# Three DMA queues for the loads of a Fourier stage, with other ring depths and pool assignments, in a Fourier, MoE and channel-mix kernel

## The chip, the cores and the metric

The kernel runs on one core of a Trainium2 chip. A core has a matrix engine (TensorE, in the profile PE, its weight loads PEld), a vector engine (VectorE, DVE), a scalar engine (ScalarE, ACT), GpSimd (POOL) and a sync engine (SyncE, SP). DMAs are issued from the instruction streams of SP, ACT or POOL; an issue sits in that stream in order, with the waits in front of it. The metric is the device time of one execution in microseconds (us), the lower the better.

## What is computed

The reference, cut to what matters (x is 4 x 3072 x 256, all in float32):

```python
X = rfft(x, axis=1)                          # along the 3072 positions
Yr = Xr @ w_r - Xi @ w_i + b_r               # 256 x 256 complex channel mix
Yi = Xr @ w_i + Xi @ w_r + b_i
Yr, Yi = soft_threshold(Yr, 0.01), soft_threshold(Yi, 0.01)
x = irfft(Yr + 1j * Yi, axis=1)              # float32
h = x @ w_in                                 # 256 -> 2048
x = (h - tanh(h)) @ w_out                    # 2048 -> 256
xk, xr = mu_k * x + (1 - mu_k) * x_prev, mu_r * x + (1 - mu_r) * x_prev
out = sigmoid(xr @ w_r2) * (relu(xk @ w_k) ** 2 @ w_v)
```

The MoE weights arrive in float64; the kernel converts them to float32 on the core.

## The kernel before

The program has three stages. The **transform** (the first fifth) does rfft, channel mix, threshold and irfft for four batches. The 3072-point transform is split into 96 x 32. For one batch it runs as follows, with the letters used below.

- **A**: eight tiles `x` (96 x 1024, 384 KB each, `load_x`) are multiplied with the 96-point matrix `f_sb`; ACT copies the result from PSUM into a tile `at` (line 464), which a DMA stores to DRAM as `adr` (line 467). In batch 0 the product is one plain float32 matmul per half tile, in the others three matmuls of split operands (`xa`, `xb`: high and low part).
- **q**: when all eight `adr` stores of the batch have landed, twelve loads `q` (256 KB, line 474) bring the rows back in the other order.
- **T, Y, V**: twelve units (`reg_unit`). T: 4 matmuls of `q` with the twiddle table `t` into bank `g`; ACT and DVE split the result into `xh`, `xl` (lines 344, 347, 499, 500). Y: 24 matmuls with the channel weights `wh`, `wl` into bank `y`; DVE adds the bias and thresholds (lines 524 to 529), ACT and DVE split that into `zh`, `zl`. V: 6 matmuls with the table `b` into bank `v`; ACT copies them to a tile `v` (line 548), and a DMA stores it as `vdr` (line 550).
- **P** (`reg_ap`): when all twelve `vdr` stores have landed, eight loads `vp` (line 557), 64 matmuls with `e_sb`, copies to `yt` (line 567) and stores `ydr` (line 568).

Beside the units DVE converts 16 weight blocks (`reg_conv`): load `raw` (512 KB, line 607), nine integer and float operations on DVE (lines 617 to 625), a store `wdr`. The second stage (**MoE**) loads these as `ws` (line 681) and makes from them operand forms `ah`, `al` (`reg_forms`, for `w_in`) and `wh`, `wl` (`reg_weight`, for `w_out`); the third stage is the channel mix over time. Both run from about 410 us to the end with PE nearly always busy.

Nothing reorders work on the chip: each engine runs its instructions in order. The order is made beforehand by a planner (`_Plan`), a list scheduler with a fixed cost per operation, a priority per operation (numbers of `K`) and one line for all DMAs (`nbytes / 360.0` ns). Dependences that are added to an operation by hand (`o.deps.add`) move its place in the planned order; the semaphore waits of the program are derived separately, from the tiles that it reads and writes. A tile is one of `bufs` buffers of a ring in a memory pool: a writer of the next tile waits for the users of the one `bufs` before. Pools open in order on reused memory: `px` (x, at, xa, xb) must be done before `pw` opens; `pt` (q, xh, xl, tables `t`, conversion scratch) before `q1`; `pm` before `q2`; `pl` (v, vp, yt) before `q3`. Before the change the forms of `w_in` blocks 0 to 3 lie in `pw`, `q1`, `q2`, `q3`.

A DMA takes one of eight semaphores of its kind in turn (DMAHW for SP and ACT, DMASW for POOL) and waits until the DMA eight before it has landed. In this kernel all loads and stores but the tables `b` are issued from SP.

Of the kernel before, what the change touches and what calls it, by code (L numbers as in the profile page):

```python
# [8 lines left out]
F32 = mybir.dt.float32  # L9
# [10 lines left out]
NP = 24  # L20
# [78 lines left out]
PACE = (0, 0, 1, 2, 3, 4)  # L99
XB, VB = 8, 4  # L100
# [47 lines left out]
class _Plan:  # L148
# [36 lines left out]
    def run(self):  # L185
# [54 lines left out]
        while done < len(ops):  # L240
# [70 lines left out]
def fourier_moe_kernel(tc, x, w_r, w_i, b_r, b_i, w_in, w_out, mu_k, mu_r, w_k, w_v, w_rr, c_f, c_e, c_t, c_b, out, nb=B, ydump=None):  # L311
# [67 lines left out]
    groups = [(0, 2), (2, 5), (5, 10), (10, 15), (15, 20), (20, NP)]  # L379
# [55 lines left out]
    def reg_a(b):  # L435
        for c in range(8):
            a = tile_(px, [NP * 4, 4, D], F32, "at", 3)
# [29 lines left out]
            dma("sp", lambda a=a, c=c: sp.dma_start(out=adr_t[b][:, 4 * c:4 * c + 4], in_=a()), pr, [adr[b]], [a], 393216)  # L467

    def reg_q(b):
        rows = adr_t[b].rearrange("r s d -> (r s) d").rearrange("(u k r) d -> u r k d", k=2, r=128)  # L470
        for u in range(NU):
            t = tile_(pt, [128, 2, D], F32, "q", NU)
            qt[b, u] = t
            dma("sp", lambda t=t, u=u: sp.dma_start(out=t(), in_=rows[u]), base(b) + u - K["q"], [t], [adr[b]], 262144)

    def reg_unit(b, u):
        n = 2
        z0 = base(b) + u
# [4 lines left out]
        qs = qt[b, u]  # L483
# [9 lines left out]
        op("pe", 448 * n, e, z0 - K["b"], [px_], [qs] + [t_sb[g] for g, _ in ts_])  # L493
        x3 = cut(px_, lambda r: r.rearrange("p (k c) -> p k c", k=4)[:, 0:2 * n])
# [52 lines left out]
        v = tile_(pl, [128, 2, D], F32, "v", 2)  # L547
# [41 lines left out]
    EARLY = 16  # L589

    def reg_conv(i):
        src, split = raws[i]
        if i < EARLY:
            w, q, s, l = (tile_(pt, [128, n], I32, tag, k) for n, tag, k in ((1024, "raw", 1), (512, "cq", 2), (512, "cs", 1), (512, "cl", 1)))
# [8 lines left out]
        def load():  # L603
# [3 lines left out]
            sp.dma_start(out=o, in_=src)  # L607
# [7 lines left out]
        dma("sp", load, pr, [raw[0]], [], 524288, after=[qt[0, NU - 1].writers[0] if i < EARLY else yload[int(K["l0"] + K["l1"] * (i - EARLY))]])  # L615
# [427 lines left out]
```

## Time and profile before

| | |
|---|---|
| median of 3 runs | 2035.78 us (2031.39 to 2036.15) |
| profiled execution | 2031.64 us, span in the trace 2029.9 us |
| PE busy | 1975.9 us (97%) |
| DVE, ACT busy | 1599.1 us (79%), 1479.3 us (73%) |
| DMA | 162.38 MB, of which about 98 MB in the first 400 us |

How to read it: a matmul that waits counts as idle time of PE, and its granted clock (PEclk, 1.00 is 2.4 GHz, 0.50 is 1.2 GHz) says how fast the busy time goes. PE is nearly always busy in the second and third stage, so what can move the time there is only the work itself. In the transform there are idle stretches and stretches at a lower clock.

### The profile page before, as it was taken

Reading aid. Unit: us, or ns where it says so; the run is one execution under the profiler, and the core shown is the slowest. Engines: PE = TensorE matmul, PEld = TensorE weight load, DVE = VectorE, ACT = ScalarE, POOL = GpSimd, SP = SyncE. Lnnn points to the kernel's source line nnn. Section 1 sums busy time; section 2 is a strip of 40 time slices with the busy share of each in tenths; the row PEclk is TensorE's granted clock in tenths of the full one; section 3 lists DMA queues with packets and bytes.
Section 4 is the critical chain, followed back from the end, with each engine's and each line's share of the span. In section 5 each row is a group of like instructions: output and inputs, shape, how many; then the busy total and the mean of one; then the engine's idle time right before and its main releaser. Section 6 shows DMA issues by size and latency. Waiting matters only on the chain.

```text
span 2029.9 us, 36670 instructions
## 1 busy us (share of the span) xinstructions
PE 1975.9 (97%) x13760; PEld 1834.6 (90%) x13760; DVE 1599.1 (79%) x3107; ACT 1479.3 (73%) x3166; POOL 3.7 (0%) x11
## 2 busy tenths in 40 slices
PE   5989999999999999999999999999999999999998
PEld 2989999888888888888888888888999999999998
DVE  0789875687888878787878797778988888888885
ACT  2647575677777777777777777778877777777774
POOL 0000000000000000000000000000000000000000
PEclk7999999799999999999999999999999999999999
DMA  9998865621101101010101020000111111112101
GB/s 246 276 288 276 293 217 163 186 72 34 37 28 41 46 26 37 21 48 22 48 22 37 21 84 32 22 11 23 58 47 47 47 46 47 48 47 55 49 22 32
DMA packets 98106, 162.38 MB, mean 80 GB/s; under 512 B 11559, under 2 KB 57735, under 8 KB 97927
## 3 DMA queue, kind: packets, MB, share of 16 engines
q1 hardware_dynamic: 97062, 156.89, 25.2%
q0 software_dynamic: 864, 3.15, 0.6%
q8 instruction: 108, 1.77, 0.4%
q14 instruction: 72, 0.58, 0.1%
HBM read 90.52 MB, written 69.47 MB: 79 GB/s over the span
## 4 chain that ended last, share of the span: by engine, by line
PE 87%; DMA 6%; DVE 4%; ACT 2%; issue 1%; SPq 1%; DVEq 0%; ACTq 0%
PE v L318 38%; PE y L318 19%; PE g L318 16%; PE a L318 14%; DMA vdr<-v 1%; DMA x<-in_x_dram 1%; DVE hs L831 1%; DVE hs L790 1%; DMA ydr<-yt 1%; DVE yl L347 1%; DMA out_dram<-ob 1%; DMA adr<-at 1%; DVE gl L347 1%; DMA yr<-ydr 0%; DMA q<-adr 0%
## 5 line engine op out<-in xcount | busy, mean ns | idle before, releaser
L344 ACT ACTIVATE gh<-hs 128x512 fp32r<-128x512 f32 x504 | 316.9, 629 | 138.8 <-PE v L318 130.4
L347 DVE TENSOR_TENSOR gl<-hs,gh 128x512 fp32r<-128x512 f32 x504 | 344.9, 684 | 78.5 <-ACT gh L344 77.6
L787 ACT ACTIVATE p<-g 128x256 f32<-128x256 f32 x864 | 318.5, 382 | 92.6 <-PE g L318 74.0
L831 DVE TENSOR_TENSOR hs<-hs,th 128x512 f32<-128x512 f32 x384 | 264.2, 689 | 124.0 <-ACT th L830 117.2
L318 PE MATMUL v<-gh,wl 128*128 128x512 f32 x768 | 302.9, 394 | 0.0
L318 PE MATMUL v<-gh,wh 128*128 128x512 f32 x768 | 302.2, 393 | 0.0
L318 PE MATMUL v<-gl,wh 128*128 128x512 f32 x768 | 301.2, 392 | 0.0
L830 ACT ACTIVATE th<-hs 128x512 f32<-128x512 f32 x384 | 241.1, 630 | 74.6 <-DVE hs L790 70.7
L790 DVE TENSOR_TENSOR hs<-y,p 128x256 f32<-128x256 f32 x588 | 241.5, 420 | 39.9 <-PE y L318 29.6
L318 PE MATMUL v<-ah,gh 128*128 128x256 f32 x768 | 217.4, 283 | 1.1 <-DVE ob L995 1.0
L318 PE MATMUL v<-al,gh 128*128 128x256 f32 x768 | 217.0, 283 | 0.0
L318 PE MATMUL v<-ah,gl 128*128 128x256 f32 x768 | 217.0, 283 | 0.0
L318 PE MATMUL g<-yh,ah 128*128 128x256 f32 x648 | 184.5, 285 | 1.5 <-ACT p L787 1.5
L318 PE MATMUL g<-yh,al 128*128 128x256 f32 x648 | 183.1, 282 | 0.0
L318 PE MATMUL g<-yl,ah 128*128 128x256 f32 x648 | 183.0, 282 | 0.0
L318 PEld LDWEIGHTS v<-gl,wh 128*128 128x128 f32 x768 | 144.3, 188 | 32.7
L318 PEld LDWEIGHTS v<-gh,wh 128*128 128x128 f32 x768 | 145.0, 189 | 17.9
L318 PEld LDWEIGHTS v<-gh,wl 128*128 128x128 f32 x768 | 144.7, 188 | 16.3
L318 PE MATMUL y<-yh,ah 128*128 128x256 f32 x496 | 150.2, 303 | 3.6 <-DVE hs L790 1.6
L318 PEld LDWEIGHTS v<-ah,gh 128*128 128x128 f32 x768 | 146.2, 190 | 1.7 <-DVE ob L995 1.7
L318 PEld LDWEIGHTS v<-al,gh 128*128 128x128 f32 x768 | 146.4, 191 | 0.0
L318 PEld LDWEIGHTS v<-ah,gl 128*128 128x128 f32 x768 | 146.2, 190 | 0.0
(171 smaller groups left out, 4884.6 us busy)
## 6 DMA issues: line engine op xcount, KB each, us to landing
x<-in_x_dram SPq DMA_DIRECT2D x32, 384.0 KB, 7.2
adr<-at SPq DMA_DIRECT2D x32, 384.0 KB, 3.6
q<-adr SPq DMA_DIRECT2D x48, 256.0 KB, 5.6
vdr<-v SPq DMA_DIRECT2D x48, 256.0 KB, 4.1
vp<-vdr SPq DMA_DIRECT2D x32, 384.0 KB, 5.7
ydr<-yt SPq DMA_DIRECT2D x64, 192.0 KB, 4.5
yr<-ydr SPq DMA_DIRECT2D x24, 512.0 KB, 4.1
xdr<-x SPq DMA_DIRECT2D x24, 512.0 KB, 3.1
```

The costliest lines, as they stand in the source:

```text
L318: pe.matmul(out=o, lhsT=l, rhs=r, start=st, stop=en, **kw)
L344: op("act", c_act(n, psum), lambda: act.activation(out=o[1](), in_=i[1](), func=ACTF.Copy), prio, [o[0]], [i[0]])
L347: op("dve", c_dve(n), lambda: dve.tensor_tensor(out=o[1](), in0=i[1](), in1=h[1]().bitcast(F32), op=ALU.subtract), prio, [o[0]], [i[0], h[0]])
L787: op("act", c_act(HK, True), lambda: act.activation(out=o(), in_=p()[:, 0:HK], func=ACTF.Copy), prio, [o], [p])
L790: op("dve", c_dve(HK), lambda: dve.tensor_tensor(out=t()[:, half * HK:half * HK + HK], in0=p()[:, 0:HK], in1=s(), op=ALU.add), prio, [t], ...
L830: op("act", c_act(CK, False), lambda th=th, hs=hs: act.activation(out=th(), in_=hs(), func=ACTF.Tanh), z0, [th], [hs])
L831: op("dve", c_dve(CK), lambda th=th, hs=hs: dve.tensor_tensor(out=hs(), in0=hs(), in1=th(), op=ALU.subtract), z0, [hs], [th])
```

## The change

- **Queues.** The loads of `w_r`, `w_i`, biases, `e_sb` and the tables `t` go from SP to POOL, beside the tables `b`. The `adr` stores of batch 0 go from SP to ACT. The raw loads of the 16 conversions go from SP to POOL.
- **Gates.** The planner holds each table load back by a matmul two units ahead (`first_mm`), and the first ones by readers of `x` tiles; the raw loads are held back until loads `q` of batches 1 to 3 instead of the last `q` of batch 0.
- **Order of units.** Unit 1 runs before unit 0 (unit 0 has four extra ACT operations). The table groups are cut accordingly.
- **Ring depths.** `x` 8 to 6 buffers, `at` 3 to 7, `v` 2 to 4.
- **Pools.** The conversion scratch moves from `pt` to `px`. The forms of `w_in` blocks 0 to 3 lie in `pw`, `pw`, `q1`, `q2`; the `w_out` blocks 0 to 2 in `pw` (before `q1`, `q1`, `q2`). Some later tiles move by one pool likewise.
- **Planner.** A DMA is planned at 290 instead of 360 bytes per ns.

```diff
-PACE = (0, 0, 1, 2, 3, 4)
-XB, VB = 8, 4
+XB, VB, AB = 6, 4, 7
+UNITS = (1, 0) + tuple(range(2, NU))
...
-                line = max(line, o.end + 650.0) + o.nbytes / 360.0
+                line = max(line, o.end + 650.0) + o.nbytes / 290.0
...
-    groups = [(0, 2), (2, 5), (5, 10), (10, 15), (15, 20), (20, NP)]
+    groups = [(2, 4), (0, 2), (4, 6), (6, 10), (10, 14), (14, 18), (18, NP)]
...
-        t = tile_(pl, [128, 2, D], F32, "v", 2)
+        t = tile_(pl, [128, 2, D], F32, "v", 4)
...
-        dma("sp", lambda t=t, w=w: sp.dma_start(out=t(), in_=w.rearrange(...)), -90, [t], [], 262144)
+        dma("pool", lambda t=t, w=w: pool.dma_start(out=t(), in_=w.rearrange(...)), -90, [t], [], 262144)
...
-        dma("sp", lambda: sp.dma_start(out=t_sb[n](), in_=c_t[:, g0:g1]), g0 / 2 - 60 + n, ...)
+        dma("pool", lambda: pool.dma_start(out=t_sb[n](), in_=c_t[:, g0:g1]), g0 / 2 - 60 + n, ...)
...
-            a = tile_(px, [NP * 4, 4, D], F32, "at", 3)
+            a = tile_(px, [NP * 4, 4, D], F32, "at", AB)
...
-            dma("sp", lambda a=a, c=c: sp.dma_start(out=adr_t[b][:, 4 * c:4 * c + 4], in_=a()), pr, ...)
+            q_, e_ = ("sp", sp) if b else ("act", act)
+            dma(q_, lambda a=a, c=c, e_=e_: e_.dma_start(out=adr_t[b][:, 4 * c:4 * c + 4], in_=a()), pr, ...)
...
-            w, q, s, l = (tile_(pt, [128, n], I32, tag, k) for ...)
+            w, q, s, l = (tile_(px, [128, n], I32, tag, k) for ...)
...
-            sp.dma_start(out=o, in_=src)
+            (pool if i < EARLY else sp).dma_start(out=o, in_=src)
...
-        dma("sp", load, pr, [raw[0]], [], 524288, after=[qt[0, NU - 1].writers[0] if i < EARLY else ...])
+        dma("pool" if i < EARLY else "sp", load, pr, [raw[0]], [], 524288, after=[qt[divmod(RAW0 + i * RAW1 // 4, NU)].writers[0] if i < EARLY else ...])
...
-        load_b[n].deps.add(xt[0, PACE[n]][0].readers[0])
-        if n > 1:
-            load_t[n].deps.add(qt[0, (groups[n][0] - 4) // 2].writers[0])
...
+                p = UNITS.index(g0 // 2)
+                for o, c in ((load_t[n], 4), (load_b[n], 6)):
+                    o.deps.add(first_mm[0, p - 2] if p > 1 else xt[0, c][0].readers[0])
...
-        win[q] = reg_forms((pw, q1, q2, q3)[q], str(q), 2 * q, P2 - K["win"] + 2 * q)
+        win[q] = reg_forms((pw, pw, q1, q2)[q], str(q), 2 * q, P2 - K["win"] + 2 * q)
...
-            wout[i] = reg_weight((q1, q1, q2, q2, q2, q3, q3, q3)[i], 8 + i, P2 - K["wout"] + 2 * q)
+            wout[i] = reg_weight((pw, pw, pw, q2, q2, q2, q3, q3)[i], 8 + i, P2 - K["wout"] + 2 * q)
```

Three places of the new order. First the start. The last rows of SP's loads before, down to the first loads `q` (the eight `x` and `w_r`, `w_i`, biases stand ahead of them; `t_147`, `t_152` are the first two tables `t`):

```order
L410 DMA e_sb<-in_c_e_dram 96x96
L415 DMA t_147<-in_c_t_dram 128x256
L415 DMA t_152<-in_c_t_dram 128x384
L467 DMA adr<-at 96x1024
L407 DMA bias<-in_b_i_dram 64x256
L409 DMA bias_137<-in_b_i_dram 63x256
L467 DMA adr<-at 96x1024 x7
L474 DMA q<-adr 128x2x256 x6
```

In the changed kernel SP from its first load on:

```order
L385 DMA f_sb<-in_c_f_dram 96x128
L398 DMA x<-in_x_dram 96x1024 x8
L475 DMA q<-adr 128x2x256 x12
L555 DMA vdr<-v 128x2x256
L396 DMA x<-in_x_dram 96x1024 x6
```

ACT in the changed kernel, from the first copy of A on (`wh` is made of `w_r`):

```order
L464 ACTIVATE at<-a 96x512 x2
L468 DMA adr<-at 96x1024
L464 ACTIVATE at<-a 96x512 x9
L468 DMA adr<-at 96x1024 x2
L424 ACTIVATE wh<-v 128x2x256
L468 DMA adr<-at 96x1024 x2
```

And POOL in the changed kernel, the end of its table loads and the first raw loads, with their waits:

```order
L417 DMA b_525<-in_c_b_dram 128x1024 [waits DMASW1_49]
L415 DMA t_535<-in_c_t_dram 128x512 [waits DMASW2_49]
L417 DMA b_628<-in_c_b_dram 128x1536 [waits DMASW3_49]
L415 DMA t_636<-in_c_t_dram 128x768 [waits DMASW4_49]
L613 DMA raw<-in_moe_w_in_dram 128x1024 [waits DMASW5_49]
L613 DMA raw<-in_moe_w_in_dram 128x1024 [waits DMASW6_49,DMASW5_49,DVE_49]
```

The stores stand in ACT's stream now, the first behind the first tile, the second behind eleven half tiles; the loads `x` of batch 1 stand behind the first `vdr` store. The table loads wait for the turn of their semaphore only, not for a matmul; the raw loads after the first one wait for DVE, which empties their one buffer.

Second, PE from the last A of batch 3 on. Before (the numbers are buffers):

```order
L318 MATMUL a_3156<-xb_3135,fh_106 128x512
L318 MATMUL y_3118<-wh_168,xh_2994 128x256 x4
L318 MATMUL y_3118<-wl_170,xh_2994 128x256 x4
L318 MATMUL y_3118<-wh_168,xl_2996 128x256 x4
L318 MATMUL v_3180<-zh_3138,b10_157 128x256 x2
L318 MATMUL v_3180<-zl_3146,b10_157 128x256
```

In the changed kernel, from the last block of Y down to the first T (`g`) of batch 3; between the last A and this fence stand one V (6 matmuls) and another block of Y:

```order
L319 MATMUL y_3244<-wh_180,xh_3143 128x256 x4
L319 MATMUL y_3244<-wl_185,xh_3143 128x256 x4
L319 MATMUL y_3244<-wh_180,xl_3159 128x256 x4
L319 MATMUL v_3291<-zh_3280,b18_628 128x256 x2
L319 MATMUL v_3291<-zl_3287,b18_628 128x256
L319 MATMUL v_3291<-zh_3280,b18_628 128x256 x2
L319 MATMUL v_3291<-zl_3287,b18_628 128x256
L319 MATMUL v_3330<-zh_3315,b18_628 128x256 x2
L319 MATMUL v_3330<-zl_3324,b18_628 128x256
L319 MATMUL v_3330<-zh_3315,b18_628 128x256 x2
L319 MATMUL v_3330<-zl_3324,b18_628 128x256
L319 MATMUL g_3345<-t2_163,q_3295 128x128 x4
```

Before, seven blocks of 12 Y and three V stand between the last A and the first T; now two blocks of 12 Y and three V (of 6 matmuls each).

Third, ACT at the end of the transform. Before, from the last copy but one into `v` on (`ah_4229`, `ah_4339` are forms of `w_in` blocks 1 and 2, `wh_4312` and `wh_4336` of `w_out`; `p`, `hs` belong to the first MoE products):

```order
L548 ACTIVATE v<-v 128x512
L344 ACTIVATE zh<-t 128x512
L344 ACTIVATE ah_4229<-ws 128x256
L787 ACTIVATE p_4287<-g 128x256
L787 ACTIVATE p_4302<-g 128x256
L344 ACTIVATE ah_4229<-ws 128x256
L344 ACTIVATE wh_4312<-ws 128x512
L548 ACTIVATE v<-v 128x512
L344 ACTIVATE ah_4229<-sq 128x1024
L344 ACTIVATE wh_4336<-ws 128x512
```

In the changed kernel, where six more units are still to deliver their `zh` (`ah_3941` is block 1, `wh_3960` of `w_out`; `zh`, `xh`, `xl` are unit work):

```order
L345 ACTIVATE zh<-t 128x512
L572 ACTIVATE yt<-a 128x384
L345 ACTIVATE ah_3941<-ws 128x256
L345 ACTIVATE yh<-yr 128x512
L345 ACTIVATE wh_3960<-ws 128x512
L345 ACTIVATE ah_3941<-ws 128x256
L345 ACTIVATE xh<-g 128x4x128
L345 ACTIVATE yh<-yt_3862 128x1024
L553 ACTIVATE v<-v 128x512
```

The forms of block 1 moved from between the last copies of the transform to between its units; those of block 2 stand now where those of block 1 stood.

## Rows read from the trace of the kernel before

**Rows 1.** The page, part 1: busy us per engine and its share.

```profile
PE 1975.9 (97%) x13760; PEld 1834.6 (90%) x13760; DVE 1599.1 (79%) x3107; ACT 1479.3 (73%) x3166; POOL 3.7 (0%) x11
```

**Rows 2.** Busy time in wide stretches: stretch, length, PE, PEld, DVE, ACT, POOL, PEclk, DMA, GB/s.

```profile
60.00:200.00 140.00, 133.54 (x1008) 127.46 (x1007) 122.01 (x237) 90.36 (x190) 0.00 (x0) 0.98 0.91 278
200.00:400.00 200.00, 189.37 (x1448) 184.50 (x1446) 138.76 (x263) 120.53 (x258) 0.00 (x0) 0.93 0.68 218
400.00:1400.00 1000.00, 997.50 (x6149) 887.54 (x6148) 811.02 (x1559) 765.05 (x1616) 0.00 (x0) 1.00 0.11 37
```

**Rows 3.** The same by 10 us, the stretches with losses.

```profile
120.00:130.00 10.00, 5.90 (x31) 5.71 (x30) 7.08 (x15) 4.25 (x12) 0.00 (x0) 0.70 0.85 305
...
290.00:300.00 10.00, 7.51 (x53) 7.31 (x53) 8.44 (x17) 6.93 (x17) 0.00 (x0) 0.83 0.94 328
...
360.00:370.00 10.00, 9.09 (x75) 8.68 (x73) 8.59 (x19) 6.23 (x16) 0.00 (x0) 1.00 0.49 156
370.00:380.00 10.00, 7.05 (x32) 6.18 (x33) 8.89 (x17) 8.48 (x20) 0.00 (x0) 0.66 0.85 248
380.00:390.00 10.00, 10.00 (x49) 10.00 (x49) 4.77 (x11) 4.91 (x12) 0.00 (x0) 0.50 0.76 218
390.00:400.00 10.00, 10.00 (x60) 9.98 (x59) 4.62 (x9) 5.48 (x12) 0.00 (x0) 0.64 0.77 253
```

**Rows 4.** Timeline of the start: start us, us, engine, line, operation, count, idle before.

```profile
1.25 3.32 POOL L417 DMA_DIRECT2D b<-in_c_b_dram  x6 [0.31 <-issue]
...
13.68 1.96 PE L318 MATMUL a<-x,f_sb 96*128 96x512 f32 x4 [1.04 <-DMA x<-in_x_dram]
...
24.76 0.33 SPq L467 DMA_DIRECT2D adr<-at  x1
...
29.60 10.13 PE L318 MATMUL a<-x,f_sb 96*128 96x512 f32 x16 [13.97 <-ACT at L464]
...
43.42 2.94 SPq L474 DMA_DIRECT2D q<-adr  x6
...
46.20 3.79 PE L318 MATMUL g<-t,q 128*128 128x128 f32 x16 [6.46 <-DMA q<-adr]
...
51.83 1.01 PE L318 MATMUL y<-wh,xh 128*128 128x256 f32 x3 [1.64 <-ACT xh L504]
```

**Rows 5.** Chain of work around 105 to 125 us: start us, us, what.

```profile
105.94 1.45 PE y L318 x12
107.38 0.72 PE v L318 x6
...
117.25 6.01 DMA vdr<-v
...
124.79 2.07 PE g L318 x8
```

**Rows 6.** Waits of ACT, 60 to 340 us: total us, times, longest.

```profile
ACT v L548 <- DMA vdr<-v: 7.9, 5, 3.5
```

**Rows 7.** Chain of work around 375 us.

```profile
376.12 1.65 PE g L318 x6
```

**Rows 8.** Loads of tile b, issued by POOL.

```profile
DMA to landing us min/median/max: 5.8/13.2/20.9
```

**Rows 9.** Tile raw: reads by DVE, who waited, landing.

```profile
L611 DVE TENSOR_SCALAR cq<-raw x16: 412/426/428, 74.5 to 244.2; 128x512 int32<-128x512 int32 x16
...
  DVE cq L611: 15.8, 9
...
DMA to landing us min/median/max: 4.2/5.9/7.0
```

**Rows 10.** Issues of adr and q, 255 to 292 us.

```profile
L474 SPq DMA_DIRECT2D q<-adr x12: 359/416/938, 282.8 to 291.4; - x12
L467 SPq DMA_DIRECT2D adr<-at x7: 303/398/821, 254.8 to 278.5; - x7
...
DMA to landing us min/median/max: 3.0/5.4/5.9
```

More of the change, by code (lines that the diff above doesn't have):

```diff
@@ L466, in reg_a, with reg_unit @@
                 op("act", c_act(512, True), v, pr, [a], [p], seq=False)
-            dma("sp", lambda a=a, c=c: sp.dma_start(out=adr_t[b][:, 4 * c:4 * c + 4], in_=a()), pr, [adr[b]], [a], 393216)
+            q_, e_ = ("sp", sp) if b else ("act", act)
+            dma(q_, lambda a=a, c=c, e_=e_: e_.dma_start(out=adr_t[b][:, 4 * c:4 * c + 4], in_=a()), pr, [adr[b]], [a], 393216)
     def reg_q(b):
         rows = adr_t[b].rearrange("r s d -> (r s) d").rearrange("(u k r) d -> u r k d", k=2, r=128)
-        for u in range(NU):
+        for i, u in enumerate(UNITS):
             t = tile_(pt, [128, 2, D], F32, "q", NU)
-            qt[b, u] = t
-            dma("sp", lambda t=t, u=u: sp.dma_start(out=t(), in_=rows[u]), base(b) + u - K["q"], [t], [adr[b]], 262144)
-    def reg_unit(b, u):
+            qt[b, i] = t
+            dma("sp", lambda t=t, u=u: sp.dma_start(out=t(), in_=rows[u]), base(b) + i - K["q"], [t], [adr[b]], 262144)
+    first_mm = {}
+    def reg_unit(b, pos):
         n = 2
-        z0 = base(b) + u
+        u = UNITS[pos]
+        z0 = base(b) + pos
         px_ = bank("g")
@@ L593, in reg_conv @@
         if i < EARLY:
[L594 removed]
+            w, q, s, l = (tile_(px, [128, n], I32, tag, k) for n, tag, k in ((1024, "raw", 1), (512, "cq", 2), (512, "cs", 1), (512, "cl", 1)))
             raw, q, s, l = (w, lambda: w().rearrange("p (c t) -> p c t", t=2)), (q, q), (s, s), (l, l)
@@ L613, in ts @@
                 dve.tensor_scalar(out=o, in0=i_, scalar1=s1, scalar2=s2, op0=o0, op1=o1)
-        dma("sp", load, pr, [raw[0]], [], 524288, after=[qt[0, NU - 1].writers[0] if i < EARLY else yload[int(K["l0"] + K["l1"] * (i - EARLY))]])
+        dma("pool" if i < EARLY else "sp", load, pr, [raw[0]], [], 524288, after=[qt[divmod(RAW0 + i * RAW1 // 4, NU)].writers[0] if i < EARLY else yload[int(K["l0"] + K["l1"] * (i - EARLY))]])
         c1, c2 = c_dve(512, False), c_dve(512)
@@ L641, in fourier_moe_kernel @@
     reg_q(0)
-    for n in range(len(groups)):
-        load_b[n].deps.add(xt[0, PACE[n]][0].readers[0])
-        if n > 1:
-            load_t[n].deps.add(qt[0, (groups[n][0] - 4) // 2].writers[0])
     for b in range(nb):
-        for u in range(NU):
-            reg_unit(b, u)
+        for i in range(NU):
+            reg_unit(b, i)
+        if b == 0:
+            for n, o in enumerate(early):
+                o.deps.add(xt[0, 1 + n][0].readers[0])
+            for n, (g0, _) in enumerate(groups):
+                p = UNITS.index(g0 // 2)
+                for o, c in ((load_t[n], 4), (load_b[n], 6)):
+                    o.deps.add(first_mm[0, p - 2] if p > 1 else xt[0, c][0].readers[0])
         if b + 1 < nb:
@@ L751, in reg_t @@
         pr = P2 + 8 * c - K["t"]
-        own = pw if c % 2 == 0 else q2
+        own = pw if c % 2 == 0 else q1
         y = tile_(pw, [128, 2, CK], F32, "yr", 1)
```

29 lines of the change are left out of this document (15 added, 14 removed).

## The prediction, made before the changed kernel had run

> **What bounds the kernel now.** I read the busy line of the page first [rows 1]: PE is busy for 1975.9 of 2029.9 us, so 54 us are idle, and those are the most that better waiting can give, beside a clock that is granted below 1.00. Then the stretches [rows 2, 3]: from 400 to 1400 us PE's busy time lacks 2.5 us of 1000, and the change leaves the order of that work nearly as it was. What can move lies in the first 400 us. There the losses stand in four places.
>
> The start: the fourth tile of A is multiplied from 13.68 on, then PE waits until 29.60, because the ring `at` has three buffers and SP issues the first `adr` store only at 24.76, behind every other load in its stream; the first `q` load is issued at 43.42 and T begins at 46.20 [rows 4]. 60 to 360 us: PE is idle for 6.5 us until 200 and 10.6 from 200 to 400, less 0.9 and 2.95 at 360 to 380: 13.2 us [rows 2, 3]. One of these is spelled out in the chain: a `vdr` store of 6.01 us ends, then PE's T begins at 124.79, after the 4.1 idle us of that stretch [rows 3, 5]; ACT stood at the copy into `v`, whose ring of two was full, and waited so for 7.9 us in all [rows 6]. The clock after such gaps: 0.70 at 120 and 0.83 at 290, which costs 5.90 x 0.30 + 7.51 x 0.17 = 3.0 us [rows 3]. The end of the transform: at 370 to 380 PE is idle for 2.95 us, the clock falls to 0.66, then 0.50 and 0.64 at full busy time: 7.05 x 0.34 + 5.0 + 3.6 = 11.0 us, with 3.9 idle 14.9 [rows 3]. There the chain runs through ACT without a gap, weight forms `ah` and `wh` among it, until PE's next product at 376.12 [rows 7].
>
> **The change part by part.** *Start, three queues.* The stores of batch 0 no longer stand behind other loads, and seven `at` buffers let PE go on. What sets T now is bytes. Before, four `x` tiles had arrived by 13.68, 3.1 us each from 1.25, 126 GB/s (384 KB each), while POOL moved 3.15 MB of `b`, the last issued at 4.0 and landing 20.9 us later, 133 GB/s [rows 4, 8]. Both queues share some 259 GB/s evenly. At that share the sixth tile is there at 19.9; then the seven stores that stand behind it, 2.75 MB, take 21 us at half of the rate (end at 41) or 10.6 at the whole (30.5). I take the middle, 35, as POOL's early loads are small ones: the first `q` 8.4 us earlier than 43.42 (bounds 2.4 and 13). The gates of the table loads cost and save nothing: in the new order they wait for semaphores of POOL alone, so they run as fast as the eight semaphores let them, as the six `b` loads did at 1.25 to 4.6, although they had hand-made gates too [rows 4]. *Unit 1 first*: before, Y waited 1.64 us for the four extra ACT operations of unit 0 and went on at 51.83 [rows 4]; unit 1 runs in that gap. -1.6.
>
> *The x loads of batch 1* stand behind the first `vdr` store. After the first V there are 3.9 us of PE work (three T, two of which took 3.79 us at the low clock [rows 4] and half of that at the full one, and parts of V) before A needs `xa`, `xb`; copy, two issues, a landing of 3.1 and two splits need about 5.6. +1.7 (0 to 6, if the tile lands as late as 7 us). Queued behind that wait on PE is the whole unit work, so it counts in full.
>
> *Rings and raw loads, 60 to 360 us.* With four `v` buffers ACT waits for the store four units back, some 18 us at 4.5 per unit (two blocks of Y at 1.45, V at 0.72, T at some 0.95); the stores take up to 6.01 [rows 4, 5]. ACT's 7.9 us of waiting there go [rows 6], and with them the PE gaps behind ACT. The raw loads leave SP; POOL has nothing else to do and refills the one buffer as soon as it is read, so DVE's 15.8 us of waiting for `raw` [rows 9] should shrink. Of 13.2 + 3.0 = 16.2 us I leave 3 (bounds 0 and 8: what is late next is the round trip `vdr` to `vp`). -13.2.
>
> *The new order opens one gap.* From the last A of batch 3 to its first T lay seven blocks of 12 Y (1.45) and three V (0.72), 12.2 us; now two and three, 5.0 us [rows 5]. The round trip was: last store issued at 278.5, first `q` at 282.8, landing 5.4 later [rows 10], 9.7 us, 10.3 with the copy. The gap is 5.3 us; with the quick landing at the start (43.42 to 46.20) and a 3.0 us store it is 1.8 [rows 4, 10]. I take 4.5, and for the clock the 1.8 us that 120 to 130 showed at a gap of that size [rows 3]. +6.3.
>
> *Pools, end of the transform.* The second `w_in` block and three `w_out` blocks now have room before the units end, and the order puts their forms between the units, where ACT and DVE have gaps. Between the last V and the first P stand 8.4 us of PE work instead of 3.2 (products of the MoE at about 0.12 and 0.23), against the same round trip of about 9. But ACT's list in that stretch still sums to some 9.5 us, so it stays late by a little, and a low clock can follow short gaps too, as it did here [rows 3]. Of 14.9 us I take 8.9 (bounds 0 and 14.9). Cover for the forms is the units of batch 3; if it is not there they are late at the old place.
>
> *Nothing*: fewer `x` buffers (A of the next batch is spread over the batch, each tile needs one), 290 instead of 360 in the planner (only the order), conversions nine units later (same density beside the units: 24 units, 30 half tiles of A and two P in either order).
>
> **Sum:** -8.4 - 1.6 + 1.7 - 13.2 + 6.3 - 8.9 = -24.1 us, 2031.6 - 24.1 = 2007.5 against the profiled execution. That lies near the low end of the three runs, 4.1 below their median; for a median I add half of that, and so in the rivals: **2009.5**.
>
> **The rivals.** *A, bytes and not queues.* If the tables get their share of the line until they are all in, 11.8 MB (x 3.15, `adr` 3.15, `b` 3.15, `t` 1.57, weights and biases 0.8) pass before `q`: at 259 GB/s that is 45.6 us, `q` at 46.8, 3.4 us later than before instead of 8.4 earlier: 2021. For it: both queues had equal shares [rows 4, 8]. Against: the stores have a queue of their own. The Trainium skill, page DMA: Bandwidth & Descriptors, section Issuing engines are not separate DMA queues, says that DMAs of all issuers run on the same engines, and that several issuers save only issue time. The rows agree as far as 259 GB/s in sum go, and by that rule alone the start is this rival.
>
> *B, the end stays*: ACT remains the late one and the clock falls as before; 8.9 us are not won: 2018. For it: the clock fell in a stretch whose gaps were short.
>
> *C, all of it*: start 13, no gap at batch 3, no remainder, end 14.9: about 46 us, 1988.
>
> *D, slower: raw loads on POOL land late.* There is one buffer, and DVE runs in order, so a late block stops the units. Conversions followed each other every (244.2 - 74.5) / 15 = 11.3 us [rows 9]; less three reads of 0.42, about 10 remain. They landed in 5.9 us from SP; the `b` loads from POOL took 5.8 to 20.9, in the middle 13.2 [rows 8, 9]. At 13.2, 16 x 3.2 = 51 us of DVE waiting, of which its idle time of 18 in 140 us [rows 2] takes some 20: +31, 2040, slower than before. It decides from a landing of about 12.8. Against: the `b` loads were six in a queue, the raw loads go one at a time. The Trainium skill, page SBUF — State Buffer, section SBUF: two separate sides, warns that DVE in a two-port mode keeps GpSimd from writing descriptors, and that a DMA of about 620 ns alone took about 3100 ns. No row of the kernel before shows POOL beside a busy DVE; worked out from that page, an estimate, a landing of 5.9 would become 8.4 and still be in time.
>
> *E, start and end both fail*: A and B together, 2030, no change that can be told.
>
> **How the numbers follow.** Forecast 0.46, A 0.13, B 0.15, C 0.08, D 0.09, E 0.09. A difference of under 0.3% (6 us) can't be told from none. Faster: 0.46 + 0.13 + 0.15 + 0.08 = 0.82; same: E, 0.09; slower: D, 0.09. The range reaches from 1992, which leaves out most of C, to 2030, which takes in A, B and half of E.
>
> **What would show it.** Right: first `adr` store near 8 us, first `q` at 30 to 41, T right behind; no wait of ACT for `vdr`, none of DVE for `raw`; a gap of 2 to 5 us before the first T of batch 3; the end of the transform at a clock near 1.00. Wrong: `q` after 43 (A); a clock of 0.50 for 20 us around the last P (B); raw landings over 10 us and DVE waiting for them (D); or a gap at a place that I don't name, such as the round trip `vdr` to `vp` in batches 0 to 2, or ACT standing at an `adr` issue.

## The result, and the profile after

The changed kernel takes 2008.1 us, median of four runs (2006.93 to 2009.99); the kernel before took 2033.59 beside it (2030.95 to 2036.15). The ratio is 0.9876, 95% interval 0.9857 to 0.9894. The forecast was 2009.5 in a range of 1992 to 2030. The profiled execution takes 2006.93 us (span 2005.1), 24.7 us less than the profiled one of before (2031.64).

The sum was right; its parts were not. To see that, I use one account for all kernels: for each stretch of 10 us the idle time of PE plus its busy time times (1 minus the granted clock), summed to 410 us. It gives 64.7 us before and 37.2 after. In all fourteen kernels the span less this account lies between 1960 and 1970 us, so it is good to about 5 us. It is read from one execution of each kernel, the profiled one. By places, before and after: the start (0 to 60 us) 33.1 and 27.5, the middle (60 to 250) 12.5 and 1.7, batch 3 and its surroundings (250 to 340) 4.2 and 5.6, the end of the transform (340 to 410) 14.9 and 2.4.

The busy line of the changed kernel's page, against [rows 1]:

```profile
PE 1961.8 (98%) x13760; PEld 1822.3 (91%) x13760; DVE 1599.4 (80%) x3107; ACT 1476.9 (74%) x3166; POOL 22.9 (1%) x42
```

The wide stretches of the changed kernel, against [rows 2]; from 400 us on nothing moved, as forecast:

```profile
60.00:200.00 140.00, 138.47 (x1074) 132.67 (x1073) 112.99 (x208) 94.10 (x201) 4.31 (x7) 1.00 0.84 265
200.00:400.00 200.00, 193.18 (x1524) 186.54 (x1523) 161.54 (x321) 129.48 (x282) 5.86 (x8) 0.99 0.71 227
400.00:1400.00 1000.00, 997.83 (x6133) 887.20 (x6132) 817.58 (x1567) 768.21 (x1621) 0.00 (x0) 1.00 0.11 35
```

Stretches of 10 us, against [rows 3]. The loss at 120 is gone, one has opened at 270, and the clock at the end of the transform stays at 1.00:

```profile
120.00:130.00 10.00, 10.00 (x89) 10.00 (x87) 8.90 (x19) 5.14 (x11) 0.53 (x1) 1.00 0.87 251
270.00:280.00 10.00, 6.76 (x46) 6.02 (x45) 9.96 (x22) 3.06 (x5) 0.72 (x1) 0.93 0.86 259
280.00:290.00 10.00, 9.04 (x70) 8.85 (x69) 5.54 (x11) 4.45 (x12) 0.72 (x1) 0.90 1.07 386
...
370.00:380.00 10.00, 9.53 (x83) 9.37 (x83) 6.89 (x15) 7.26 (x17) 0.00 (x0) 1.00 0.94 310
380.00:390.00 10.00, 9.92 (x79) 9.43 (x79) 4.61 (x10) 6.76 (x18) 0.00 (x0) 1.00 0.45 166
```

The start, against [rows 4]: the first `adr` store goes out 16.8 us earlier, `q` 7.0 and T 6.5 us earlier, and POOL issues all tables and then the first raw load by 24.97:

```profile
7.96 0.35 ACTq L468 DMA_DIRECT2D adr<-at  x1
...
24.97 0.53 POOL L613 DMA_DIRECT2D raw<-in_moe_w_in_dram  x1
36.39 7.71 SPq L475 DMA_DIRECT2D q<-adr  x12
...
39.72 3.61 PE L319 MATMUL g<-t,q 128*128 128x128 f32 x16 [16.17 <-DMA q<-adr]
```

ACT has no row any more that waits for `vdr` between 60 and 340 us (7.9 us in [rows 6]). DVE still waits for `raw`, 6.4 us instead of 15.8 [rows 9], and the raw loads land in 6.2 us from POOL (median; 5.9 from SP). The waits of DVE, 60 to 340 us: total us, times, longest:

```profile
DVE cq L617 <- DMA raw<-in_moe_w_in_dram: 3.3, 2, 2.6
DVE cq L617 <- DMA raw<-in_moe_w_out_dram: 3.1, 1, 3.1
```

Up to here everything looks as the prediction told it. The experiments say otherwise.

### The profile page after: what moved, and what is told of

Its sections match the earlier page's. It is cut to its first block, busy times and chain, and to the rows that moved or that the text cites. A ratio compares the mean times of both kernels' runs of the same rounds, so it can differ in the third digit from the quotient of the medians.

```text
span 2005.1 us, 36620 instructions
## 1 busy us (share of the span) xinstructions
PE 1961.8 (98%) x13760; PEld 1822.3 (91%) x13760; DVE 1599.4 (80%) x3107; ACT 1476.9 (74%) x3166; POOL 22.9 (1%) x42
## 4 chain that ended last, share of the span: by engine, by line
PE 89%; DVE 5%; DMA 3%; ACT 2%; issue 1%; SPq 0%; ACTq 0%; DVEq 0%
PE v L319 39%; PE y L319 20%; PE g L319 17%; PE a L319 14%; DVE hs L840 1%; DVE hs L799 1%; DVE yl L348 1%; DMA x<-in_x_dram 1%; DMA adr<-at 1%; DVE gl L348 1%; DMA ydr<-yt 0%; DMA out_dram<-ob 0%; DVE zl L348 0%; DMA vp<-vdr 0%; DMA yr<-ydr 0%
```

## The experiments

Each job also ran the kernel before; "difference" is the median less that median. The ratio and its interval come from all runs and not from the medians, so a few longer runs move them (e1). "V to P" is PE work, in us at full clock, that the order puts between the last V and the first P of batches 0 to 3, worked out as in the prediction; it covers the trip from `vdr` to `vp`, the store of the last V and the load behind it, and is called the cover below. The account is by the four places named above; for e5 the profiled execution (2035.2 us) lies 9 us above the median, for e10 (2008.08) 5 below it.

| kernel | median us | difference | ratio, interval | V to P | account, sum |
|---|---|---|---|---|---|
| before | 2033.59 | | | 7.9, 10.8, 7.9, 3.2 | 33.1 12.5 4.2 14.9, 64.7 |
| after | 2008.1 | -25.5 | 0.9876 (0.9857 to 0.9894) | 11.1, 18.3, 16.4, 8.4 | 27.5 1.7 5.6 2.4, 37.2 |
| e1 pools back | 2009.03 | -23.0 | 0.9908 (0.9876 to 0.9939) | 11.1, 18.3, 20.4, 4.5 | 29.7 3.1 8.3 4.4, 45.4 |
| e2 `v` ring 2 | 2009.62 | -22.4 | 0.9892 (0.9872 to 0.9911) | 12.2, 17.2, 17.2, 7.3 | 26.2 8.7 2.6 2.8, 40.4 |
| e3 raws on SP | 2008.01 | -24.0 | 0.988 (0.9862 to 0.9899) | 10.4, 16.1, 16.4, 7.3 | 27.2 2.9 5.5 2.5, 38.1 |
| e4 tables held | 2010.45 | -21.5 | 0.9895 (0.9876 to 0.9914) | 11.1, 18.3, 16.4, 8.4 | 30.3 3.4 5.2 2.5, 41.4 |
| e5 rate 360 | 2025.87 | -7.1 | 0.9972 (0.9947 to 0.9997) | 9.3, 8.6, 9.3, 6.3 | 23.5 17.7 11.3 14.7, 67.2 |
| e6 before, rate 290 | 2011.28 | -21.7 | 0.989 (0.9868 to 0.9912) | 18.6, 11.1, 18.3, 4.5 | 29.9 10.7 2.2 6.9, 49.8 |
| e7 start back | 2010.38 | -22.6 | 0.9891 (0.987 to 0.9913) | 14.0, 15.7, 15.8, 6.6 | 29.1 7.5 2.7 4.0, 43.3 |
| e8 start only | 2015.19 | -17.7 | 0.9908 (0.9883 to 0.9933) | 10.4, 9.3, 12.5, 3.2 | 20.0 8.9 2.2 16.2, 47.3 |
| e9 360, `vp` later | 2012.36 | -23.0 | 0.9898 (0.9863 to 0.9933) | 12.5, 12.5, 13.3, 10.8 | 26.1 10.3 1.9 4.1, 42.5 |
| e10 three parts back | 2012.70 | -22.6 | 0.989 (0.9862 to 0.9919) | 13.6, 15.0, 24.0, 4.5 | 29.5 5.3 5.1 6.1, 46.0 |
| e11 before, `v` ring 4 | 2045.30 | +10.0 | 1.0046 (1.0028 to 1.0064) | 7.9, 7.9, 8.3, 3.2 | 31.8 30.7 3.9 12.0, 78.4 |
| e12 mixed rate | 2002.72 | -28.9 | 0.986 (0.9844 to 0.9877) | 11.1, 18.3, 16.4, 8.4 | 22.1 2.0 5.2 2.0, 31.4 |

### One part undone at a time: e1 to e4

e1 puts the pools of conversion scratch and weight forms back:

```diff
-        win[q] = reg_forms((pw, pw, q1, q2)[q], ...)
+        win[q] = reg_forms((pw, q1, q2, q3)[q], ...)
```

> The changed kernel (2008.1 us) with the pool moves undone: conversion scratch in pt, forms of w_in in pw, q1, q2, q3, of w_out in q1, q2, q3, the later tiles likewise; all else as changed. Theory: the end of the transform ran at full clock only because the second block of forms was made between the units. Undone, ACT is late again at the last V, PE gets gaps of 2 to 5 us there and a clock of 0.5 to 0.7 for some 20 us: plus 8 to 14 us, 2016 to 2022. Rival: the gaps and the clock went for another reason (other order by the planner's 290, conversions elsewhere): 2006 to 2011, clock near 1.00 around the last P.

e2 puts the `v` ring back to 2, e3 the raw loads back on SP:

```diff
-        v = tile_(pl, [128, 2, D], F32, "v", 4)
+        v = tile_(pl, [128, 2, D], F32, "v", 2)
```

```diff
-            (pool if i < EARLY else sp).dma_start(out=o, in_=src)
+            sp.dma_start(out=o, in_=src)
```

> The changed kernel with the v ring back at 2 buffers. Theory: ACT stands at the copy into v for stores of vdr again, 5 to 10 us in all, PE waits behind it at the batch ends with a lower clock after: plus 5 to 12 us, 2013 to 2020. Rival: it was the raw loads leaving SP that freed the stores; then ACT's wait for vdr stays under 2 us and the time at 2007 to 2011. (The planner moves the first T of batch 2 closer to its last A, 6.5 instead of 11.5 us; a wait of T for q there would show as such.)

> The changed kernel with the 16 raw loads of the conversions issued from SP as before the change, same gates. Theory: DVE waits for raw blocks some 10 to 16 us in all instead of 6.4, part of it under the saturated stretch at 250 to 290: plus 1 to 4 us, 2009 to 2012. Rival: the queue is worth more, since SP's stores and loads stand behind them again: plus 6 or more, 2014 and up. Rival 2: nothing, 2008.

e4 adds a POOL operation ahead of the later table loads that waits for ACT's last copy of A in batch 0, so that the tables can't move before:

```diff
+                    op("act", 100, lambda: act.activation(out=gsink(), in_=gate(), func=ACTF.Copy), pr, [gsink], [gate], after=[plan.ops[-1]])
+                    op("pool", 100, lambda: pool.memset(gate(), 0.0), -58, [gate])
```

> The changed kernel with the table loads from the fourth group on really held back: a small POOL instruction in front of them waits for ACT's last copy of A in batch 0 (about 24 us). Theory that bytes set the start: 3.5 MB fewer stand beside the stores of A, the first q goes out at 26 to 31 instead of 36.4, T begins at 29 to 34 instead of 39.7, and the time falls by 4 to 9 us to 1999 to 2004. Rival: the eight stores from ACT are slow by themselves (10.1 us from issue to landing): q stays at 34 to 37 and the time at 2006 to 2010. Third: the tables come too late for units 3 to 6 and PE waits for them: 2008 to 2016.

By the medians e1 to e4 cost 2.5, 3.1, 1.5 and 4.0 us (difference less after's), and their intervals overlap that of the changed kernel. The theories of e1 and e2 expected 8 to 14 and 5 to 12; that of e4 expected a gain of 4 to 9. At the rate of 290 the parts on which the prediction put 13.2 and 8.9 us are nearly free to undo. With the pools back, PE is idle for 3.6 us at 360, as the prediction had it, but the clock stays at 1.00, so only a small part of the 14.9 returns. The row of e1:

```profile
360.00:370.00 10.00, 6.39 (x38) 4.69 (x36) 9.06 (x18) 9.73 (x22) 0.00 (x0) 1.00 0.78 229
```

The median hides something here. Two of e1's five runs took 2015.45 and 2020.86 us, at a mean granted clock of 0.988 and 0.986 (0.991 to 0.993 in the other three), and two of the four runs of e10, which has the old pools too, 2016.39 and 2019.06 at 0.985; the runs of the changed kernel lie within 3.1 us. None of these four longer runs was profiled. That the clock at the end of the transform fell in them, as e1's theory had it, is possible and not shown.

e4 tells what sets T. The first `q` is issued at 31.99, 4.4 us earlier, and T still begins at 40.19 instead of 39.72: the tables now move beside the `q` loads, which land in 11.0 us (median) instead of 5.8. Timeline of e4:

```profile
31.99 12.80 SPq L484 DMA_DIRECT2D q<-adr  x10
...
40.19 2.05 PE L319 MATMUL g<-t,q 128*128 128x128 f32 x8 [11.85 <-DMA q<-adr]
...
43.96 1.41 PE L319 MATMUL g<-t,q 128*128 128x128 f32 x5 [1.73 <-DMA q<-adr]
```

So the bytes in front of T set it, not the gates.

### One number: e5 and e6

The remaining suspects were the planner's rate, and that several parts each do the same. e5 puts the number back in the changed kernel, e6 changes it alone in the kernel before:

```diff
-                line = max(line, o.end + 650.0) + o.nbytes / 290.0
+                line = max(line, o.end + 650.0) + o.nbytes / 360.0
```

> The changed kernel with one number put back: the planner again counts 360 and not 290 bytes per ns for a transfer. No instruction is added or taken out; only the order on the engines changes (PE work between the last V and the first P of batches 0 to 3 falls from 11.1, 18.3, 16.4 and 8.4 us to 9.3, 8.6, 9.3 and 6.3; between the last A and the first T of batch 3 it rises from 5.0 to 13.0). Theory O (order): the new order carries most of what was won from 60 us on, and 8 to 15 us of it are lost: 2016 to 2023 us. Theory R (redundant): rings, queue, pools and order each do enough, and a single one put back costs little: 2007 to 2011. The prediction's own costing: the rate alone is worth nothing, and the gap before T of batch 3 (6.3) goes: 2001 to 2003.

> The kernel before with one number changed: the planner counts 290 and not 360 bytes per ns. PE work between the last V and the first P of batches 0 to 3 becomes 18.6, 11.1, 18.3 and 4.5 us (7.9, 10.8, 7.9, 3.2 before), between the last A and the first T of batches 1 to 3 12.2, 2.9 and 9.4 (12.2 each before). Theory O: it wins 8 to 15 us against the kernel before (2017 to 2025), less a new gap of 3 to 5 before T of batch 2. Theory R: much the same, since order alone would do enough: 2019 to 2026. The prediction's costing: nothing won, and a gap before T of batch 2 of about 6 is new: 2032 to 2040.

e5 loses 18.4 of the 25.5 us by the differences; e6 wins 21.7 with this number alone. Theory O expected 8 to 15 in both, and theory R less in e5 and much the same as O in e6. So the order does much, and no forecast had its size. The new gap before T of batch 2 in e6 is there too: between 190 and 212 us PE waits 3.4 us for `q` and 2.6 for `zh`, and with the clock the account loses 10.0 us there (190 to 220).

What the number takes from the kernel before isn't a wait for `vp`. That wait was 0.6 us there, and P of batches 0 to 2 ran at the full clock. PE's largest wait was that of T for `xh`. In e6 it is nearly gone, although the `v` ring is still 2, and ACT waits for no `vdr` store any more from 60 to 340 us (7.9 in [rows 6]); at the end of the transform the account falls by 8.0. Which move in the order does this is not shown. PE's waits in 60 to 410 us, before:

```profile
PE g L318 <- ACT xh L499: 10.7, 5, 4.1
PE a L318 <- DMA vp<-vdr: 0.6, 1, 0.6
```

The same in e6:

```profile
PE g L318 <- DMA q<-adr: 4.3, 3, 2.3
PE g L318 <- ACT xh L499: 0.5, 2, 0.3
```

e5 shows how time is lost where the ring is 4 and the cover short. Chain of work of e5 around the first P of batch 1 (start us, us, what):

```profile
203.76 0.73 PE v L319 x6
...
205.15 2.87 DMA vdr<-v
...
208.16 5.61 DMA vp<-vdr
...
213.81 8.29 PE a L319 x48
```

The last V ends at 204.49; copy, store and load take until 213.77, 9.3 us, and there are 8.6 us of PE work for them. PE is idle for only about 1 us. But look at the clock of e5 at this place and at the first P of batches 2 and 3:

```profile
210.00:220.00 10.00, 8.92 (x64) 8.72 (x62) 9.22 (x20) 4.46 (x10) 0.72 (x1) 0.82 1.02 313
220.00:230.00 10.00, 10.00 (x48) 10.00 (x48) 1.54 (x4) 1.47 (x3) 0.00 (x0) 0.50 0.92 308
...
310.00:320.00 10.00, 10.00 (x48) 10.00 (x48) 5.19 (x10) 4.71 (x10) 0.00 (x0) 0.50 1.04 320
...
390.00:400.00 10.00, 10.00 (x49) 10.00 (x49) 4.25 (x7) 4.59 (x10) 0.00 (x0) 0.50 0.84 253
```

P runs at half the clock with PE busy all the time, 48 or 49 matmuls in 10 us (the trace has two records for each of the 64 of a P). From 210 to 230 the clock costs 1.6 + 5.0 us and the idle time 1.1. In the changed kernel the trip is no shorter, but it lies behind more work; its chain and its stretch at the same place:

```profile
207.67 0.73 PE v L319 x6
...
209.58 5.76 DMA vp<-vdr
...
215.38 6.71 PE a L319 x58
```

```profile
220.00:230.00 10.00, 10.00 (x88) 10.00 (x88) 6.13 (x14) 3.74 (x8) 0.72 (x1) 1.00 1.04 351
```

The clock also goes with the wide spread of e5: its ten runs go from 2017.11 us, at a mean granted clock of 0.991, to 2038.36, at 0.978. Only the one of 2035.2 was profiled.

### The start alone, and without it: e7 and e8

e7 puts the loads and `adr` stores of the start back on SP, with 8 `x` and 3 `at` buffers; e8 keeps the start and puts back ring, pools, queue of the raws and rate:

```diff
-            q_, e_ = ("sp", sp) if b else ("act", act)
+            q_, e_ = "sp", sp
```

> The changed kernel with the loads and adr stores of the start on SP's queue again, 8 x buffers and 3 at buffers; unit 1 still goes first, and all the rest of the change stays. The prediction's costing: 8.4 us of the gain go, less nothing: 2015 to 2018. Theory O and theory R: the same term by the loss account of the first 60 us, 33.1 before and 27.5 after, 5.6 us: 2012 to 2015.

> The changed kernel with everything but the start put back: v ring of 2, weight forms and conversion scratch in their old pools, raw loads on SP, planner rate 360; what stays is the start on three queues, 6 x and 7 at buffers, unit 1 first and the later conversions. PE work between the last V and the first P is 10.4, 9.3, 12.5 and 3.2 us. Theory O: the start's 5.6 us and little else: 2024 to 2029 us. Theory R (parts redundant, none is left here): the same, 2024 to 2029. The prediction's costing: start, unit swap and x wait together 8.3 us: 2023 to 2026. If it comes out below 2018, neither rate, ring, pools nor queue carries the middle and the end, and the later conversions or the changed start do.

e7 misses all its forecasts on the good side: 2.9 us lost. e8 misses on the good side too: -17.7 where 4 to 10 were expected. Its start costs only 20.0 us, 13 less than before, although it is the same code as in the changed kernel (27.5). In e8 two units of T stand ahead of the second V, and PE goes on behind the first V; in the changed kernel half of the second V stands first and waits there for ACT's `zh`, and T for `xh`. Timeline of the changed kernel:

```profile
53.18 0.72 PE L319 MATMUL v<-zh,b 128*128 128x256 f32 x2 [1.78 <-ACT zh L345]
...
54.28 3.10 PE L319 MATMUL g<-t,q 128*128 128x128 f32 x16
...
58.90 1.16 PE L319 MATMUL g<-t,q 128*128 128x128 f32 x8 [1.16 <-ACT xh L504]
```

The expectation of e8 named 2018 as the time below which neither rate, ring, pools nor queue would carry the middle and the end; 2015.19 lies below it. The account says where: of the 17.4 us that it falls against the kernel before, 13.1 lie in the start and 5.6 between 60 and 340; the end is 1.3 worse. So the middle and the end still lose 25.1 us in e8, against 4.1 in the changed kernel, and something that was put back does carry them. The later conversions and the swap of units 0 and 1 stay in e8, and no run tries either alone.

So beside the other parts the rate of 290 buys the middle and gives part of the start back. e8's end falls to 0.50 as before (V to P 3.2), 16.2 us.

### One place of the order: e9

If the cover in front of P is the cause, it must be enough to lengthen that cover alone. e9 is e5 with one more number in the planner, `late`, which is 4000 ns for the loads of `vp` and 0 for all else:

```diff
-                o.lat = line + 950.0 - o.end
+                o.lat = line + 950.0 - o.end + o.late
...
+            plan.ops[-1].late = 4000.0
```

> The kernel of e5 (planner rate 360) with one more number: in the planner alone, the load of vp is counted 4 us longer. No instruction is added or taken out. PE work between the last V and the first P of batches 0 to 3 becomes 12.5, 12.5, 13.3 and 10.8 us (9.3, 8.6, 9.3, 6.3 in e5); between the last A and the first T 12.2, 12.2, 10.8. Theory O, now sharpened to one place (what the rate of 290 buys is work in front of P, behind which the trip vdr to vp hides; the clock that falls after PE waited there is what costs): losses after 60 us fall from 44 to under 10 while the start keeps e5's 23.5: 1998 to 2006 us, faster than the changed kernel. Rival O2 (the rate of 290 helps by other moves in the order, such as where conversions and T stand): it stays near e5, 2018 to 2030. Theory R has no say here. The prediction's costing: nothing but order, no change against e5.

It wins 15.9 us over e5 by the differences (three runs at 2008.88 to 2013.16 us, one at 2024.93), and the account after 60 us falls from 43.7 to 16.3, more than that because e5's profiled execution was one of its longest. P waits for `vp` no more (4.0 us in e5), and P of batches 2 and 3 keeps the clock (that of batch 1 loses it for 7 us at 232):

```profile
310.00:320.00 10.00, 9.92 (x86) 9.76 (x86) 8.67 (x15) 8.19 (x17) 0.00 (x0) 1.00 1.03 366
...
390.00:400.00 10.00, 10.00 (x81) 9.66 (x81) 4.69 (x10) 7.53 (x18) 0.00 (x0) 1.00 0.40 139
```

The forecast of 1998 to 2006 is missed by 6 us, because other waits stay. The planner moves other work too when it counts `vp` later, so e9 shows that the gain comes with the longer cover, not that nothing else has a part in it. PE's waits, 60 to 410 us:

```profile
PE a L320 <- ACT yt L574: 4.6, 4, 2.3
PE g L320 <- ACT xh L505: 4.1, 5, 1.3
```

### Parts together, and one alone: e10 and e11

e10 undoes e1, e2 and e3 together, which tells whether they stand in for each other; e11 makes the `v` ring 4 in the kernel before, with both lines of e2 turned round.

> The changed kernel with the v ring at 2, weight forms and scratch in their old pools and raw loads on SP, all three at once; rate 290, the start and unit 1 first stay. PE work between the last V and the first P is 13.6, 15.0, 24.0 and 4.5 us. Theory O: order does it, the three parts together are worth no more than the short cover of the last batch: 2009 to 2014 us. Theory R (ring, pools and queue stand in for each other, so that undoing one shows nothing): the three together cost 8 to 15: 2016 to 2023. The prediction's costing: 13.2 and 8.9 us go, 2026 to 2030.

> The kernel before with one number changed, the v ring 4 and not 2; PE work between the last V and the first P stays 7.9, 7.9, 8.3 and 3.2 us. The prediction's costing: ACT's wait for vdr goes and with it most of 13.2 us, 2018 to 2024. Theory O: the ring lies off the path while the order in front of P stays short: 2028 to 2034, no change.

e10: the three together cost 2.9 us by the differences. With the new start and the rate of 290 they don't replace each other; they carry little.

The table holds one more comparison. e8 and e10 differ by the rate alone, and with the three parts back and the new start in place it is worth 4.9 us by the differences, not 18 or 22: in e10 the middle and the end lose 13.7 us less, the start and batch 3 12.4 more. In the other direction, e5 is e8 with the three parts at the rate of 360, and there they make the kernel 10.6 us slower. The parts don't add: the start alone, with the later conversions, wins 17.7, the rate alone 21.7, both together (e10) 22.6.

e11 is the surprise: the term that I put first in the middle makes the kernel before 10 us **slower**. PE's waits in 60 to 410 us, of e11:

```profile
PE g L318 <- ACT xh L499: 7.8, 7, 1.6
PE a L318 <- DMA vp<-vdr: 6.9, 3, 3.8
```

In the kernel before these were 10.7 and 0.6 us. ACT waits for no `vdr` store any more, yet most of T's wait for `xh` stays, and a wait for `vp` is new. At batch 0 PE waits less in front of T (1.2 us idle from 120 to 130 instead of 4.1) and is ready for P at 134.1 instead of 136.8. And the trip is longer: from the end of the last V to the first landed `vp` it takes 13.1 us, where before it took 7.1 (store 2.2, load 4.2). Why its transfers take longer is not shown. Chain of e11 at batch 0:

```profile
125.66 5.83 DMA vdr<-v
...
131.55 6.23 DMA vp<-vdr
...
137.82 2.24 PE a L318 x9
```

And P then runs at the low clock, where before it ran at the full one from its first matmul at 136.8 on:

```profile
130.00:140.00 10.00, 4.64 (x29) 4.25 (x29) 8.62 (x19) 2.31 (x6) 0.00 (x0) 0.79 0.80 211
140.00:150.00 10.00, 10.00 (x49) 10.00 (x49) 3.53 (x6) 3.65 (x8) 0.00 (x0) 0.50 0.67 210
```

Less waiting in front of T came back as waiting in front of P, at a higher price.

### One rate for the start, another behind it: e12

```diff
-                line = max(line, o.end + 650.0) + o.nbytes / 290.0
+                line = max(line, o.end + 650.0) + o.nbytes / (360.0 if s < 60000.0 else 290.0)
```

> The changed kernel, whose planner counts 360 bytes per ns for what it starts in its first 60 us and 290 from there on. No instruction is added or taken out. The first 14 groups of PE's order stand as in e5 (two units of T ahead of the second V), PE work between the last V and the first P is the changed kernel's: 11.1, 18.3, 16.4 and 8.4 us, between the last A and the first T of batch 3 again 5.0. Theory O in its sharpened form (each stretch is set by its own cover): the start's loss falls from 27.5 to e5's 23.5, the stretches from 60 us on keep the changed kernel's 9.7: 2003 to 2006 us, and so ahead of both kernels. Rival: a start that is 4 us earlier only arrives earlier at waits that transfers set later, as the wider v ring alone did: 2007 to 2012.

2002.72 us, every run (2002.28 to 2003.51) below every run of the changed kernel (2006.93 to 2009.99), in another job: 5.4 us by the medians, 3.4 by the differences. The two never ran side by side, and the intervals of their ratios overlap. The start's loss is 22.1, everything behind it stays as in the changed kernel, as forecast. Its stretches at 50, 270 and 390 us:

```profile
50.00:60.00 10.00, 9.40 (x67) 8.31 (x68) 6.20 (x12) 6.58 (x14) 0.00 (x0) 1.00 0.70 190
270.00:280.00 10.00, 6.08 (x32) 5.27 (x31) 8.58 (x19) 3.06 (x6) 1.44 (x2) 0.83 1.00 331
...
390.00:400.00 10.00, 10.00 (x62) 8.94 (x61) 7.60 (x16) 6.89 (x16) 0.00 (x0) 1.00 0.01 2
```

## Why the prediction was right, and where it was not

**What failed: "290 instead of 360 in the planner (only the order)", costed at nothing.** Alone it wins 21.7 us (e6), without it 18.4 are lost (e5); with ring, pools and raw loads put back it is worth 4.9 (e8 to e10). So it can't be priced by itself. I had worked out PE's work between V and P for the last batch only, 3.2 and 8.4 us; for batches 0 to 2 it went from 7.9, 10.8 and 7.9 to 11.1, 18.3 and 16.4, which the same count of the order would have shown, against a trip that the prediction itself put at about 9 us. What I listed as "wrong" if it came, a gap at the trip `vdr` to `vp` in batches 0 to 2, is what the changed kernel would have without this number: PE waits there in e5 and e11, and P of batches 1 and 2 in e5, of 0 and 1 in e11, runs at the low clock. In the kernel before this place cost next to nothing (0.6 us).

**Middle, -13.2 for rings and raw loads.** The account gives -10.8 from 60 to 250, so the size fits. The loss was read rightly too: ACT's wait for `vdr` is gone in the changed kernel, and PE's for `xh` is 1.2 us instead of 10.7. What takes them away was not: the rate alone does so with the ring at 2 (e6), the ring undone costs 3.1 us and ACT still waits for no `vdr`, the raws' queue costs 1.5, both with the pools 2.9 (e2, e3, e10), and the ring alone makes the kernel 10 slower (e11). The step that failed is "ACT's 7.9 us of waiting there go, and with them the PE gaps behind ACT": with the ring alone the wait goes, 7.8 of the 10.7 us of gaps stay, and 6.9 come at P.

**End, -8.9 for pools.** The account gives -12.5; the pools undone cost 2.5 us by the median (e1; two of its five runs lie 6 and 12 above that median). Rival B, ACT late and the clock falling, came with the short cover of e8 and the rate of e5; with the old pools in the profiled executions the clock didn't fall there in e1, and in e10 for 7 us ahead of P. Part of this I had in the sum, as cover of 8.4 instead of 3.2, but I credited it to the weight forms.

**Start, -8.4, -1.6 and +1.7.** `q` was forecast at 35 and came at 36.39, 7.0 us earlier than before; T is 6.5 us earlier, the account 5.6. The mechanism stands (`q` goes out earlier because its stores do), the size is a little smaller, and the wait of +1.7 came at the place but for ACT's `zh` and `xh`, not for `x`: it belongs to the order (e8, e12). Undoing the start costs only 2.9 us (e7), where alone it wins 17.7 (e8); why so little is not shown. The swap of units, -1.6, was undone in no run. Rival A is true in part: e4 shows that held tables take the line from `q` instead. On that, the Trainium skill, page DMA: Bandwidth & Descriptors, section Issuing engines are not separate DMA queues, says that DMAs of all issuers share the same engines; e4 agrees, with `q` landing in 11.0 us instead of 5.8 beside the tables. Yet the sum wasn't fixed at the 259 GB/s that the rival's 2021 was worked out from: from 20 to 30 us the kernel before moved 311 and the changed one 403.

**Gap in batch 3, +6.3.** Idle time and clock at 270 to 290 sum to 5.6 us, at the forecast place. The cause that I named, the trip `adr` to `q`, is not what PE waited for, 260 to 292 us:

```profile
PE v L319 <- ACT zh L345: 2.5, 1, 2.5
PE g L319 <- ACT xh L504: 1.0, 1, 1.0
PE v L319 <- DVE zl L348: 0.7, 1, 0.7
```

DVE is busy for 9.96 of 10 us there, with conversions between the operations of the units. That too many conversions fall there is argued from this trace, not tried by a run; e6 to e9, whose orders differ there, lose 1.9 to 2.7 us in that stretch (250 to 340).

**Rival D, raws from POOL land late.** False: 6.2 us in the middle, 8.1 at most beside a busy DVE, where 12.8 was the point from which it would decide. Only the first, issued at 24.97 among the loads of the start, took 13.8, and DVE first read it at 116.3.

So the time was met in part by luck: the size of what lay idle was read rightly from [rows 2, 3], and how much of it would go; what would take it away was not, and a ring that costs time alone stood in the sum as its largest gain.

## What to carry to other kernels

In an order made by a planner, one number that looks like bookkeeping can be worth most of a change or little of it, by what stands beside it (21.7, 18.4 and 4.9 us here): before costing it at nothing, count for every round trip through DRAM, in every batch, the work that lies between its two ends in both orders. Undo each part alone, and also do it alone: ring, pools, raw loads and start were nearly free to undo, the ring was harmful alone and the start good for 17.7 us, while the profile of after agreed with a wrong story. And price a wait by what runs behind it: in e5, 1.1 us of idle time came to 7.7 where P followed at half the clock.

## What the runs showed of the hardware

- **A low clock that stays while PE is busy.** From 60 us on, the profiled executions of the fourteen kernels have eight stretches of 13.8 to 24.0 us at a clock of 0.50: one in the kernel before (from 373, [rows 3]), three in e5, one in e8, three in e11. In each the first P begins between 2.4 us before the fall and 4.5 us after it, PE had been idle for 1.1 to 3.5 of the 8 us before the fall, and the clock rises again while P still runs. The cover between V and P was 9.3 us or less in all eight; 22 of the 56 blocks P had so little, and of the other 34 none fell for that long. PE is busy for 10.00 of 10 us within them, with 48 or 49 matmuls. The falls elsewhere lasted up to 10.2 us. The Trainium skill, page TensorE: Matmul & The Clock Gate, Part 1, says that activity releases the throttle; in these rows PE was busy throughout and the clock stayed at 0.50. What it is in P that goes with the low clock stays open, and idle time alone doesn't decide it: in e1, PE was idle for 3.6 us at 360 to 370, in waits of 1.4 us or less, and the clock stayed at 1.00.
- **DMA of POOL beside a busy DVE.** In the changed kernel the issues of the raw loads took 528 to 789 ns, and the fifteen from 117 us on landed in 4.4 to 8.1 us. Five of the issues, and the landing of those between 100 and 260 us:

```profile
L613 POOL DMA_DIRECT2D raw<-in_moe_w_out_dram x5: 722/724/789, 208.3 to 247.6; - x5
...
DMA to landing us min/median/max: 4.4/6.2/8.1
```

  DVE was busy for 9.96 of 10 us from 270 on, when POOL issued one of them in 0.72 us, which landed in 4.4. The stall of which the Trainium skill, page SBUF — State Buffer, section SBUF: two separate sides, warns is not seen in any run here: from 60 us on no raw load from POOL took over 9.1 us to land. Whether DVE ran in the two-port mode then, the traces don't say.
- **More bytes per us at the start.** The first 60 us moved 261 GB/s before, 290 after and 313 in e12; with the start back on SP (e7) 249, with the tables held (e4) 270. The order differs between these kernels too, so the number of queues alone isn't shown to be the cause.
